# An attention block with a SwiGLU network behind it: matmuls that read their moving operand as two halves in turn

## The chip, the cores and the metric

The kernel runs on one core of a Trainium2 chip. A core has TensorE (matmuls, which read SBUF and write PSUM), VectorE, ScalarE and GpSimd, which work on their own and wait for each other through semaphores, and queues that issue DMAs. The metric is the time of one execution on the device, in microseconds. Times given are medians of several runs; the profile is of one execution.

## The reference

Two blocks follow each other. The first lets 32 inducing points attend to a sequence, and then the sequence to the result; the second is an RMS norm with a gated network.

```python
# x: (4, 12416, 128), inducing: (32, 128)
def mab(q, kv):
    s = (q @ kv.transpose(0, 2, 1)) / sqrt(128)
    a = exp(s - s.max(-1, keepdims=True))
    a /= a.sum(-1, keepdims=True) + 1e-09
    return a @ kv
h = mab(inducing, x)           # (4, 32, 128)
y = mab(x, h)                  # (4, 12416, 128), then (49664, 128)

# w_gate, w_val: (128, 1536), w_out: (1536, 128)
xn = y / sqrt(mean(y * y, -1) + 1e-06) * rms_g
g, val = xn @ w_gate, xn @ w_val
out = (g * (1 / (1 + exp(-g))) * val) @ w_out
```

All is float32.

## The kernel before

The output of the attention is never formed. Since y = a @ h, the product xn @ w_gate is a @ (h * rms_g @ w_gate), with the norm's factor put into the weights a. For each of the 4 batches the kernel makes the two small products of h with w_gate and w_val, 32 rows each. It stacks them four times (two upper and two lower parts of the numbers) into the tiles `sg` and `sv`, 128 x 1536, of type float32r. The attention weights, turned so that tokens lie along the columns, are likewise split into an upper and a lower part, and `gather` copies these into the tile `a` of a unit: 128 partitions by T tokens.

A **unit** is T tokens: 512 in 80 of the 100 units, 480 in 16, 256 in 4. There are 25 units in a batch. `ffn(b, u)` makes the steps of one unit, and each unit has 12 **slots**, one for each 128 of the 1536 hidden columns. A slot `j` (function `slot`) does:

- the gate product (L732), `sg` stationary and `a` moving, into one of five PSUM banks `gv`; ScalarE takes SiLU of it into `silu` (L740);
- the value product (L743) into another of these banks; VectorE multiplies both (L749) into the factor, either in place in PSUM or into a tile `u` in SBUF.

The factor then goes to the output product with `w_out`, which adds up over the 12 slots in the PSUM tile `acc`. It goes one of two ways, chosen in advance for each slot by a table of letters (619 `s`, 200 `d`, 381 dots):

- **plain** (a dot): one float32 matmul `acc += wo[j] x u` (`project`, L669). The trace has two records for each such product.
- **split** (`s` or `d`): the factor is split by ScalarE, VectorE and GpSimd (L714, L715, L718, L719, L723, L724 in `three`) into float32r parts `hi`, `lo` and `d`, and `project3` makes three float32r matmuls: two into the PSUM tile `u3` (L690 and L692), one into `acc` (L669). When the last split product of a unit is done, ScalarE evicts `u3` (L695) into `o`.

At the end of a unit `finish` adds `acc` and `o` (L677, on VectorE), then VectorE turns the sum in blocks of 32 x 32 (L680), and `store` sends the four groups of 32 partitions to the output by DMA. In the two units without a split product there is no L695 and no L677, and L680 reads `acc` itself.

The kernel keeps eight PSUM banks: five `gv`, two `acc`, one `u3`. All loops are unrolled. The order of instructions on each engine is written out by hand: tables say at which slot a step of the next batch's attention is placed, which of the plain (`p`) and split (`t`) output products are issued within which slot, which of the five banks a product takes, and which buffer a factor takes. A scheduler does not reorder anything.

Of the kernel before, what the change touches and what calls it, by code (L numbers as in the profile page):

```python
# [13 lines left out]
AF = mybir.ActivationFunctionType  # L14
ALU = mybir.AluOpType
# [3 lines left out]
P = 128  # L19
R = 4  # L20
# [3 lines left out]
def kernel(  # L24
# [45 lines left out]
    nc = tc.nc  # L70
# [3 lines left out]
    NJ = F // P  # L74
# [421 lines left out]

    split_of, moving = {}, {}

    def seam(b, s):

        st = {}
        n, rows = per2[s], rows2[s]
        w = n * m
        engine = nc.gpsimd if b or s else nc.vector

        def numbers(name):
            return small.tile([P, 16], F32, name=name)[rows, 0:n]

        def turn_a():
            eT = st["eT"] = worker([P, 512], F32, "eT")  # L510
            nc.vector.transpose(out=eT[rows, 0:w], in_=sc[b][rows, cols2[s]])

        def square():
            ps = st["ps"] = bank()
            nc.tensor.matmul(ps[rows, 0:w], gram[b][rows, rows], st["eT"][rows, 0:w], start=True, stop=True)  # L515

        def turn_z():
            ps = st["ps"]
            z = st["z"] = worker([P, 512], F32, "z")[:, 0:n * m].rearrange("p (t m) -> p t m", m=m)
            flat = z[rows, :, :].rearrange("p t m -> p (t m)")  # L520
            nc.vector.tensor_tensor(out=flat, in0=ps[rows, 0:w], in1=st["eT"][rows, 0:w], op=ALU.mult)
            nc.vector.transpose(out=flat, in_=flat)

        def scale():
            ms = numbers("ms")
            nc.vector.reduce_sum(out=least[rows, 0:n, 0], in_=st["z"][rows, :, :], axis=AX.X)
            nc.vector.reduce_max(out=ms, in_=least[rows, 0:n, :], axis=AX.X)
            st["ms"] = ms

        def root():  # L530
            rs = st["rs"] = numbers("rs")
            nc.gpsimd.tensor_tensor(out=rs, in0=st["ms"], in1=mhalf[rows, 0:n], op=ALU.pow)

        def apply():
            rs, a = st["rs"], weights(b, s)
            engine.tensor_tensor(out=a, in0=a, in1=rs.unsqueeze(2).to_broadcast((rs.shape[0], n, m)), op=ALU.mult)

        def turn_b():
            aT = st["aT"] = worker([P, 512], F32, "aT")
            nc.vector.transpose(out=aT[rows, 0:w], in_=sc[b][rows, cols2[s]])  # L540

        def split():
            aT = st["aT"]
            hi, lo = split_of[b, s] = [halves.tile([P, 512], F32R, name=k) for k in ("hi", "lo")]
            if b or s:
                nc.scalar.copy(out=hi[rows, 0:w], in_=aT[rows, 0:w])
            else:
                nc.vector.tensor_copy(out=hi[rows, 0:w], in_=aT[rows, 0:w])
            engine.tensor_tensor(out=lo[rows, 0:w], in0=aT[rows, 0:w], in1=hi[rows, 0:w].bitcast(F32), op=ALU.subtract)

        return [turn_a, square, turn_z, scale, root, apply, turn_b, split]
# [98 lines left out]
    def weight_of(kind, j):  # L650
        if j >= NK:
            return kws["last"][:, kind * (NJ - NK) + j - NK, :]
        n = kind * NK + j
        return kws["first"][:, n, :] if n < half + NK else kws["more"][:, n - half - NK, :]

    def ffn(b, u):

        s, q = units[u]
        T = per2[s] * m
        a = moving.pop((b, u))  # L660
        sg, sv = stacks[b]
        acc = ps_acc.tile([P, 512], F32, name="acc")
        nk = sum((b, u, j) in kinds for j in range(NJ))
        st = {"left": NJ, "k": nk}
        if nk:
            st["o"] = None

        def project(lhsT, rhs):
            nc.tensor.matmul(acc[:, 0:T], lhsT, rhs, start=st["left"] == NJ, stop=st["left"] == 1)  # L669
            st["left"] -= 1  # L670
            if not st["left"]:
                soon(1, finish)

        def finish():
            o = st["o"] if nk else outp.tile([P, 512], F32, name="o")
            if nk:
                nc.vector.tensor_tensor(out=o[:, 0:T], in0=acc[:, 0:T], in1=o[:, 0:T], op=ALU.add)  # L677

            def turn():
                nc.vector.transpose(out=o[:, 0:T], in_=(o if nk else acc)[:, 0:T])  # L680
                soon(2, lambda: store(o))

            soon(1, turn)

        def project3(j, where):
            if st["k"] == nk:
                st["u"] = ps_u.tile([P, 512], F32, name="u3")
            ups = st["u"]
            hi, lo, d = (one[:, 0:T] for one in kws["sets"][where])
            nc.tensor.matmul(ups[:, 0:T], weight_of(0, j), hi, start=st["k"] == nk, stop=False)  # L690
            st["k"] -= 1
            nc.tensor.matmul(ups[:, 0:T], weight_of(1, j), lo, start=False, stop=not st["k"])  # L692
            if not st["k"]:
                o = st["o"] = outp.tile([P, 512], F32, name="o")
                nc.scalar.activation(o[:, 0:T], ups[:, 0:T], AF.Copy, scale=1.0 + 2.0 ** -12)  # L695
            project(weight_of(2, j), d)
            give_back(where, idle, leaving)

        def store(o):
            if s == full:  # L700
                d = out[ds(b * N + start[s], P * per[s]), :].rearrange("(i w) c -> i w c", i=m)
            else:
                d = of(out, b, s)[q]
            for k in range(R):
                queue = nc.scalar if (b, u) == flat[-1] and k % 2 else nc.sync
                queue.dma_start(out=d[:, :, ts(k, m)], in_=o[ts(k, m), 0:T].rearrange("p (t c) -> p t c", c=m))

        def three(j, t):

            where = idle.pop(0)  # L710
            hi, lo, d = (one[:, 0:T] for one in kws["sets"][where])
            v, kind = t[:, 0:T], kinds[b, u, j]
            if kind == "sums":
                nc.scalar.activation(hi, v, AF.Copy, scale=(1.0 - 2.0 ** -13) * 2.0 ** -12)  # L714
                nc.vector.scalar_tensor_tensor(out=lo, in0=hi.bitcast(F32), scalar=-4096.0, in1=v,  # L715
                                               op0=ALU.mult, op1=ALU.add)
            else:
                nc.scalar.activation(d, v, AF.Copy, scale=1.0 - 2.0 ** -13)  # L718
                nc.gpsimd.tensor_tensor(out=lo, in0=v, in1=d.bitcast(F32), op=ALU.subtract)  # L719

            def rest():
                if kind != "sums":
                    nc.scalar.activation(hi, d.bitcast(F32), AF.Copy, scale=2.0 ** -12)  # L723
                nc.gpsimd.tensor_tensor(out=d, in0=hi.bitcast(F32), in1=lo.bitcast(F32), op=ALU.subtract)  # L724
                kara.append(lambda: project3(j, where))

            soon(1, rest)

        def slot(j, products, steps, tanh):
            products(0)  # L730
            g = bank()
            nc.tensor.matmul(g[:, 0:T], sg[:, ts(j, P)], a[:, 0:T], start=True, stop=True)  # L732
            sl = silp.tile([P, 512], F32, name="silu")
            if tanh:

                nc.scalar.activation(sl[:, 0:T], g[:, 0:T], AF.Tanh, scale=0.5)
                nc.vector.scalar_tensor_tensor(out=sl[:, 0:T], in0=sl[:, 0:T], scalar=1.0, in1=g[:, 0:T],
                                               op0=ALU.add, op1=ALU.mult)
            else:
                nc.scalar.activation(sl[:, 0:T], g[:, 0:T], AF.Silu)  # L740
            products(1)
            v = bank()
            nc.tensor.matmul(v[:, 0:T], sv[:, ts(j, P)], a[:, 0:T], start=True, stop=True)  # L743
            t = v if kinds.get((b, u, j)) == "sums" else up.tile([P, 512], F32, name="u", tag=f"u{factors.pop(0)}")
            if tanh:
                nc.vector.scalar_tensor_tensor(out=t[:, 0:T], in0=sl[:, 0:T], scalar=0.5, in1=v[:, 0:T],
                                               op0=ALU.mult, op1=ALU.mult)
            else:
                nc.vector.tensor_tensor(out=t[:, 0:T], in0=sl[:, 0:T], in1=v[:, 0:T], op=ALU.mult)  # L749
            steps()  # L750
            if (b, u, j) in kinds:
                soon(1, lambda: three(j, t))
            else:
                plain.append(lambda: project(wo[:, j, :], t[:, 0:T]))

        return slot
# [550 lines left out]
```

## Time and profile before

| what | value |
|---|---|
| median of 3 runs | 1573.27 us (1573.14 to 1574.48) |
| the profiled execution, its span from the first to the last instruction | 1571.7 us |
| TensorE busy | 1559.7 us, 99% of the span |
| VectorE busy | 1461.7 us, 93% |
| GpSimd busy | 1432.5 us, 91% |
| ScalarE busy | 1302.4 us, 83% |
| granted TensorE clock | 1.000 |
| DMA engines, mean over the span | 72 GB/s |

The profiled execution is known by its span alone; the runs, timed from outside, stand 1.6 us above it at the median. Matmuls are pipelined: the duration of a matmul's record overlaps the next one, so that the pace is read from the distance between the ends of consecutive records, or from the pieces of the chain of waits, which follow one another without overlap. "PEld" is the load of a stationary operand, which lies beside the matmuls. A name such as `xn` can stand for another tile that uses the same buffer: the rings of `hi`, `lo` and `d` lie in buffers that the input used at first, and later in those of `sg` and `sv`.

### The profile page before, as it was taken

The page shows a single profiled execution, that of the slowest core. Times are in us where ns is not written, and L with a number is a line of the kernel's source. Part 1 is how long each engine was busy: PE and PEld are TensorE (multiplying, and loading weights), DVE is VectorE, ACT ScalarE, POOL GpSimd, SP SyncE. Part 2 cuts the span into 40 slices and gives each one's busy share as a digit, 9 for nine tenths or more (in the row PEclk, how much of TensorE's full clock was granted, in tenths as well). Part 3 has the DMA queues.
Part 4 walks back from the last instruction along what each step waited for, and adds up shares of the span by engine and source line. Part 5 has one row for each costly group of instructions (what it writes and reads, how often), then busy time and mean ns, then how long its engine had stood idle before and what let it go on. Part 6 is the DMA issues. An engine that isn't in the chain of part 4 may idle for free.

```text
span 1571.7 us, 26132 instructions
## 1 busy us (share of the span) xinstructions
PE 1559.7 (99%) x7141; PEld 1108.5 (71%) x7141; DVE 1461.7 (93%) x2546; ACT 1302.4 (83%) x2501; POOL 1432.5 (91%) x1158
## 2 busy tenths in 40 slices
PE   9999999999999999999999999999999999999998
PEld 6566667767776667776677667776777777777777
DVE  6999999899999998999999999899999999999997
ACT  5687888788888889887988888978798888888886
POOL 1379999999999999999999999899989999999997
PEclk9999999999999999999999999999999999999999
DMA  7355526334453242634444323353212122121221
GB/s 283 86 87 92 102 40 132 84 65 87 66 93 61 37 91 39 132 81 85 71 77 81 55 60 71 81 109 73 51 36 39 35 36 36 33 37 37 40 39 27
DMA packets 389331, 112.58 MB, mean 72 GB/s; under 512 B 365088, under 2 KB 369728, under 8 KB 386624
## 3 DMA queue, kind: packets, MB, share of 16 engines
q1 hardware_dynamic: 388592, 110.83, 35.4%
q8 instruction: 57, 0.93, 0.3%
q14 instruction: 90, 0.74, 0.2%
q10 hardware_dynamic: 592, 0.08, 0.0%
HBM read 53.95 MB, written 27.00 MB: 52 GB/s over the span
## 4 chain that ended last, share of the span: by engine, by line
PE 97%; DVE 1%; ACT 1%; POOL 0%; issue 0%; DMA 0%; SPq 0%; ACTq 0%; POOLq 0%; DVEq 0%
PE acc L669 31%; PE gv L732 18%; PE gv L743 17%; PE u L690 12%; PE u L692 12%; PE gv L341 3%; PE gv L515 1%; PE gv L390 1%; PE gv L808 1%; PE acc L191 0%; PE gv L469 0%; ACT silu L740 0%; PE gv L483 0%; DVE u L749 0%; DMA out_dram<-o 0%
## 5 line engine op out<-in xcount | busy, mean ns | idle before, releaser
L724 POOL TENSOR_TENSOR xn<-xn,xn 128x512 fp32r<-128x512 f32 (+2 forms) x626 | 776.2, 1259 | 47.2 <-DVE xn L715 13.7
L740 ACT ACTIVATE silu<-gv 128x512 f32<-128x512 f32 (+2 forms) x1186 | 683.7, 587 | 135.3 <-PE gv L732 123.6
L743 PE MATMUL gv<-a,sv 128*128 128x512 f32 (+2 forms) x1188 | 566.3, 477 | 0.0
L732 PE MATMUL gv<-a,sg 128*128 128x512 f32 (+2 forms) x1188 | 481.8, 406 | 0.6 <-ACT silu L740 0.3
L749 DVE TENSOR_TENSOR gv<-silu,gv 128x512 f32<-128x512 f32 (+2 forms) x616 | 412.4, 674 | 35.1 <-PE gv L743 14.1
L749 DVE TENSOR_TENSOR u<-silu,gv 128x512 f32<-128x512 f32 (+2 forms) x570 | 370.5, 656 | 32.4 <-PE gv L743 15.2
L669 PE MATMUL acc<-u,wo 128*128 128x512 f32 (+2 forms) x762 | 370.3, 576 | 0.0
L714 ACT ACTIVATE xn<-gv 128x512 fp32r<-128x512 f32 (+2 forms) x472 | 278.3, 590 | 56.3 <-DVE gv L749 39.4
L715 DVE SCALAR_TENSOR_TENSOR xn<-xn,gv 128x512 fp32r<-128x512 f32 (+2 forms) x472 | 312.9, 663 | 9.4 <-ACT xn L714 4.5
L732 PEld LDWEIGHTS gv<-a,sg 128*128 128x128 f32 x1188 | 223.6, 188 | 132.7 <-issue 32.6
L743 PEld LDWEIGHTS gv<-a,sv 128*128 128x128 f32 x1188 | 223.8, 188 | 106.7 <-issue 26.6
L690 PE MATMUL u<-xn,xn 128*128 128x512 f32 (+2 forms) x599 | 242.3, 405 | 0.0
L669 PE MATMUL acc<-xn,more 128*128 128x512 f32 (+2 forms) x599 | 232.0, 387 | 0.0
L719 POOL TENSOR_TENSOR xn<-u,xn 128x512 fp32r<-128x512 f32 (+2 forms) x154 | 192.4, 1249 | 5.4 <-ACT xn L718 5.3
L669 PEld LDWEIGHTS acc<-u,wo 128*128 128x128 f32 x762 | 142.5, 188 | 43.4 <-issue 16.9
L690 PEld LDWEIGHTS u<-xn,xn 128*128 128x128 f32 x599 | 112.7, 188 | 32.9 <-issue 7.2
L724 POOL TENSOR_TENSOR sg<-sg 128x512 fp32r<-128x512 f32 (+2 forms) x97 | 124.8, 1286 | 5.0 <-DVE sg L715 1.4
L669 PEld LDWEIGHTS acc<-xn,more 128*128 128x128 f32 x599 | 112.5, 188 | 23.5
L724 POOL TENSOR_TENSOR sv<-sv 128x512 fp32r<-128x512 f32 (+1 forms) x96 | 123.5, 1286 | 5.9 <-DVE sv L715 3.2
L692 PE MATMUL u<-xn,more 128*128 128x512 f32 (+2 forms) x304 | 117.3, 386 | 0.0
L692 PE MATMUL u<-xn,xn 128*128 128x512 f32 (+2 forms) x295 | 114.0, 386 | 0.0
L718 ACT ACTIVATE xn<-u 128x512 fp32r<-128x512 f32 (+2 forms) x154 | 95.3, 619 | 12.6 <-DVE u L749 5.2
(231 smaller groups left out, 1921.2 us busy)
## 6 DMA issues: line engine op xcount, KB each, us to landing
out_dram<-o SPq DMA_DIRECT2D x320, 64.0 KB, 2.0
xT<-in_x_dram SPq DMA_DIRECT2D x60, 256.0 KB, 3.8
xn<-in_x_dram SPq DMA_DIRECT2D x60, 256.0 KB, 5.1
a<-hi SPq DMA_DIRECT2D x156, 64.0 KB, 2.0
a<-lo SPq DMA_DIRECT2D x156, 64.0 KB, 2.0
xn<-in_x_dram SPq DMA_DIRECT2D x5, 1024.0 KB, 9.0
xn<-w SPq DMA_DIRECT2D x18, 256.0 KB, 3.0
out_dram<-o SPq DMA_DIRECT2D x64, 60.0 KB, 2.0
```

What stands on the lines that cost most here:

```text
L669: nc.tensor.matmul(acc[:, 0:T], lhsT, rhs, start=st["left"] == NJ, stop=st["left"] == 1)
L690: nc.tensor.matmul(ups[:, 0:T], weight_of(0, j), hi, start=st["k"] == nk, stop=False)
L692: nc.tensor.matmul(ups[:, 0:T], weight_of(1, j), lo, start=False, stop=not st["k"])
L714: nc.scalar.activation(hi, v, AF.Copy, scale=(1.0 - 2.0 ** -13) * 2.0 ** -12)
L715: nc.vector.scalar_tensor_tensor(out=lo, in0=hi.bitcast(F32), scalar=-4096.0, in1=v, op0=ALU.mult, op1=ALU.add)
L718: nc.scalar.activation(d, v, AF.Copy, scale=1.0 - 2.0 ** -13)
L719: nc.gpsimd.tensor_tensor(out=lo, in0=v, in1=d.bitcast(F32), op=ALU.subtract)
L724: nc.gpsimd.tensor_tensor(out=d, in0=hi.bitcast(F32), in1=lo.bitcast(F32), op=ALU.subtract)
L732: nc.tensor.matmul(g[:, 0:T], sg[:, ts(j, P)], a[:, 0:T], start=True, stop=True)
L740: nc.scalar.activation(sl[:, 0:T], g[:, 0:T], AF.Silu)
L743: nc.tensor.matmul(v[:, 0:T], sv[:, ts(j, P)], a[:, 0:T], start=True, stop=True)
L749: nc.vector.tensor_tensor(out=t[:, 0:T], in0=sl[:, 0:T], in1=v[:, 0:T], op=ALU.mult)
```

## The change

Two functions are new. `halves_in_turn` reorders the access pattern of a moving operand: instead of columns 0, 1, 2, ... of T it reads 0, T/2, 1, T/2 + 1, ... . All gate, value and output products use it, plain and split. The result of a product therefore lies in that order in PSUM, and SiLU and the split keep it. The output product reads its operand, which is already in that order, as two halves in turn again, so that the columns of `acc` and `u3` stand as four quarters of the tokens in turn. `in_order` reads such a PSUM tile with a step of four columns, so that it comes out in the order of the tokens: in L695 for `u3`, in L677 for `acc`. In the two units without split products a copy from `acc` to `o` is new, and L680 then reads `o`. The tables of the order of work stay as they are.

```diff
--- before.py
+++ after.py
@@ -496,6 +496,14 @@
 
     split_of, moving = {}, {}
 
+    def halves_in_turn(ap):
+
+        return ap.rearrange("p (h n) -> p n h", h=2)
+
+    def in_order(ap):
+
+        return ap.rearrange("p (n q) -> p q n", q=R)
+
     def seam(b, s):
 
         st = {}
@@ -666,18 +674,21 @@
             st["o"] = None
 
         def project(lhsT, rhs):
-            nc.tensor.matmul(acc[:, 0:T], lhsT, rhs, start=st["left"] == NJ, stop=st["left"] == 1)
+            nc.tensor.matmul(acc[:, 0:T], lhsT, halves_in_turn(rhs), start=st["left"] == NJ, stop=st["left"] == 1)
             st["left"] -= 1
             if not st["left"]:
                 soon(1, finish)
 
         def finish():
             o = st["o"] if nk else outp.tile([P, 512], F32, name="o")
+            whole = o[:, 0:T].rearrange("p (q n) -> p q n", q=R)
             if nk:
-                nc.vector.tensor_tensor(out=o[:, 0:T], in0=acc[:, 0:T], in1=o[:, 0:T], op=ALU.add)
+                nc.vector.tensor_tensor(out=whole, in0=in_order(acc[:, 0:T]), in1=whole, op=ALU.add)
+            else:
+                nc.vector.tensor_copy(out=whole, in_=in_order(acc[:, 0:T]))
 
             def turn():
-                nc.vector.transpose(out=o[:, 0:T], in_=(o if nk else acc)[:, 0:T])
+                nc.vector.transpose(out=o[:, 0:T], in_=o[:, 0:T])
                 soon(2, lambda: store(o))
 
             soon(1, turn)
@@ -687,12 +698,13 @@
                 st["u"] = ps_u.tile([P, 512], F32, name="u3")
             ups = st["u"]
             hi, lo, d = (one[:, 0:T] for one in kws["sets"][where])
-            nc.tensor.matmul(ups[:, 0:T], weight_of(0, j), hi, start=st["k"] == nk, stop=False)
+            nc.tensor.matmul(ups[:, 0:T], weight_of(0, j), halves_in_turn(hi), start=st["k"] == nk, stop=False)
             st["k"] -= 1
-            nc.tensor.matmul(ups[:, 0:T], weight_of(1, j), lo, start=False, stop=not st["k"])
+            nc.tensor.matmul(ups[:, 0:T], weight_of(1, j), halves_in_turn(lo), start=False, stop=not st["k"])
             if not st["k"]:
                 o = st["o"] = outp.tile([P, 512], F32, name="o")
-                nc.scalar.activation(o[:, 0:T], ups[:, 0:T], AF.Copy, scale=1.0 + 2.0 ** -12)
+                nc.scalar.activation(o[:, 0:T].rearrange("p (q n) -> p q n", q=R), in_order(ups[:, 0:T]), AF.Copy,
+                                     scale=1.0 + 2.0 ** -12)
             project(weight_of(2, j), d)
             give_back(where, idle, leaving)
 
@@ -729,7 +741,7 @@
         def slot(j, products, steps, tanh):
             products(0)
             g = bank()
-            nc.tensor.matmul(g[:, 0:T], sg[:, ts(j, P)], a[:, 0:T], start=True, stop=True)
+            nc.tensor.matmul(g[:, 0:T], sg[:, ts(j, P)], halves_in_turn(a[:, 0:T]), start=True, stop=True)
             sl = silp.tile([P, 512], F32, name="silu")
             if tanh:
 
@@ -740,7 +752,7 @@
                 nc.scalar.activation(sl[:, 0:T], g[:, 0:T], AF.Silu)
             products(1)
             v = bank()
-            nc.tensor.matmul(v[:, 0:T], sv[:, ts(j, P)], a[:, 0:T], start=True, stop=True)
+            nc.tensor.matmul(v[:, 0:T], sv[:, ts(j, P)], halves_in_turn(a[:, 0:T]), start=True, stop=True)
             t = v if kinds.get((b, u, j)) == "sums" else up.tile([P, 512], F32, name="u", tag=f"u{factors.pop(0)}")
             if tanh:
                 nc.vector.scalar_tensor_tensor(out=t[:, 0:T], in0=sl[:, 0:T], scalar=0.5, in1=v[:, 0:T],
```

## The prediction

> **What bounds the kernel now.** I read the shares of the chain of waits first, then a table of windows, the chain piece by piece, and the groups by form.
>
> ```profile
> span 1571.7 us, 26132 instructions
> ...
> PE 97%; DVE 1%; ACT 1%; POOL 0%; issue 0%; DMA 0%; SPq 0%; ACTq 0%; POOLq 0%; DVEq 0%
> PE acc L669 31%; PE gv L732 18%; PE gv L743 17%; PE u L690 12%; PE u L692 12%; PE gv L341 3%; PE gv L515 1%; PE gv L390 1%; PE gv L808 1%; PE acc L191 0%; PE gv L469 0%; ACT silu L740 0%; PE gv L483 0%; DVE u L749 0%; DMA out_dram<-o 0%
> ```
>
> The chain is TensorE nearly everywhere, and 90% of it is the five lines that the change edits. Who comes next is read from one window, from the first full units to the tail:
>
> ```profile
> core 0: us, PE busy (x) PEld busy (x) DVE busy (x) ACT busy (x) POOL busy (x), PEclk, DMA share, GB/s
> 100.00:1540.00 1440.00, 1439.26 (x6368) 1026.81 (x6367) 1355.12 (x2318) 1216.65 (x2331) 1374.83 (x1097) 1.00 0.35 66
> ```
>
> In these 1440 us GpSimd is idle for 65 us, VectorE for 85, ScalarE for 223. The clock is full, so no gain can come from there. How fast the products go is seen in the chain, where each piece lasts until the next one takes over:
>
> ```profile
> 56.30 1.72 PE acc L669 x4
> ...
> 602.33 0.23 PE gv L743
> 602.56 0.23 PE gv L732
> 602.79 0.23 PE u L690
> 603.03 0.23 PE u L692
> 603.26 0.23 PE acc L669
> ...
> 605.12 0.86 PE acc L669 x2
> ```
>
> Two speeds. A plain fp32 product (L669 on wo) is two records of 0.43 us. A record streams its operand twice (a product is four passes), so a pass of 512 columns takes 0.215. An fp32r product streams it once and takes 0.23. From the ends of consecutive records in the trace (medians): fp32 records 429 ns at 512 columns, 402.5 at 480 and 215.5 at 256, hardly varying (428 to 430 at 512). The fp32r ones take 232.5, 217 and 118, and vary (225 to 240 at 512). So the array shows 214.5, 201 and 108 ns a pass, and fp32r falls 18, 16 and 10 ns short: 8%, in proportion to the columns. It is the same on all five lines (231.5 to 232.9) and whether VectorE, ScalarE, GpSimd or DMAs are busy beside it or not (232.0 to 233.1). So the loss lies in the fp32r pass itself. An fp32r pass takes a new word at every step of the array, a plain record one at every second step. I read the loss as the moving operand arriving too slowly: a reading, not shown.
>
> **The change, part by part.**
>
> *The reads.* The marks in the kernel give 819 split products of 1200, 381 plain. fp32r passes: 2 x 1200 gate and value, 3 x 819 split, 4857 in all. No instruction is added; only the order in which the moving operand is read changes. 80 of 100 units have 512 columns, 16 have 480, 4 have 256, so the shortfall is 0.80 x 18 + 0.16 x 16 + 0.04 x 10 = 17.4 ns a pass, and 4857 x 17.4 ns = 84 us of TensorE time. That is the gain's end. The other end: if the words came at one per two steps, as a plain record takes them, a pass would cost what a plain record does, 429: (196.5 x 0.80 + 185.5 x 0.16 + 97.5 x 0.04) = 191 ns more a pass, 927 us in all. No matmul of the trace reads its operand with a hop, so these rows are bounds. The row of another engine nearest to it is on VectorE:
>
> ```profile
> L715 DVE SCALAR_TENSOR_TENSOR xn<-xn,gv 128x512 fp32r<-128x512 f32 x370 | 251.0, 678 | 6.2 <-ACT xn L714 2.3
> ...
> L677 DVE TENSOR_TENSOR o<-acc,o 128x512 f32<-128x512 f32 x78 | 53.2, 683 | 0.0
> ...
> L279 DVE SCALAR_TENSOR_TENSOR we<-sc,we 128x512 int32<-128x512 int32 x6 | 4.1, 684 | 0.0
> ```
>
> L279 reads every second word of its source and takes 684 ns; L715, the same operation on adjacent words, takes 678. A hop alone costs VectorE nothing there, at half the array's pace or less. Two facts make me take the gain's end: a pass that falls short in proportion to its length with neighbours idle or busy is held up by its own run of addresses, and the change alters just that run; and the one hop on view is free. It is the weakest step here.
>
> Plain records: 762 x 0.43 us already run at the array's pace with a word per two steps, so I cost their new order at nothing; if a hop takes more than two steps, that cover is gone and every nanosecond per pass costs 1.5 us over their 1524 passes.
>
> *A rule against, and one for.* The row: an fp32r pass of adjacent words is 8% slow. The Trainium skill, "SBUF — State Buffer", section "Door 1: The DMA port swizzle", says that a read wants at least two hits on a 16-byte line and pays each time that it moves to another line. In the new order every word lies in another line than the one before, so by the rule alone passes get slower and the sum goes to the rivals below; no run here shows it for TensorE. "Vector Engine (DVE) Microarchitecture Reference", section "5.2 Measured stream behaviour on trn2", speaks for both: 1.73 ns a column where a source of VectorE hops at every word, but the full rate where one stream alternates between two regions, which is this pattern. By its first figure, my estimate is 886 ns a pass and a kernel near 4,700 us; by its second, the forecast.
>
> *What of the 84 us is kept.* A faster TensorE asks the others for more in the same time. In the window it would need 1440 - 83 = 1357 us, VectorE 1355, GpSimd 1375: three engines level, in an order written by hand, with five PSUM banks for gate and value. GpSimd's 1375 caps the gain at 65. What is late next is a split operand from L724 (1297 ns on GpSimd) or a factor from L749. No row gives the share kept; I take half of 65, 33 us, since all three would then still stand at 96 to 98% of 1407 us.
>
> *The evictions.* 98 of 100 units leave `acc` through L677 (683 ns) and `u` through L695 on ScalarE (608 ns); both now read every fourth word of PSUM. By L279 that costs nothing, which I take as the nearest row; the upper end is a doubling: 98 x 0.68 = 67 us on VectorE against its 85 idle, 98 x 0.6 = 59 on ScalarE against 223. Behind L695 waits the next unit's first L690, since `u` has one PSUM bank: now 6.2 us, 19 times, in the table of waits; a doubling could make it 98 x 0.6 = 59 more, of which I allow 27 in the range. The two units without split products (all plain, at the start) get a VectorE copy before their transpose, 2 x 0.69 = 1.4 us, hidden by `acc`'s second bank. Their transpose read from PSUM took 710 ns against 703 from SBUF: nothing.
>
> **Sum.** 1571.7 - 33 = 1538.7 us of span. The runs' median, 1573.27, stands 1.6 above the profiled span, and I carry that: 1540.3. With 65 kept it is 1508; with 33 kept and the evictions' 27 lost, 1567.
>
> **Rivals.**
>
> *The order of reading makes no difference.* Then fp32r stays at 232.5 and only the evictions are left: 1573, to 1600 with their 27 us. For it: a loss that is the same whatever runs beside it could as well be a clock ratio of the port, which no address order cures. Against: such a loss should not vary by 15 ns between passes. 14 in 100, half of it within 0.2% (3.2 us, about what a measurement of this kernel can tell from no change).
>
> *Each change of place costs (slower).* If the 18 ns are the price of moving on in memory, the new order moves more often. Its place is the moving read of the 4857 passes, and no slack hides it, since TensorE is the bound: each further 17.4 ns costs 84 us, and it decides from 0.7 ns a pass (3.2 us). With the loss at two to four times I get 1658 to 1826; the factors are my estimate, without a row. For it: proportion to length and the scatter. Against: L279's free hop. 18 in 100.
>
> *One word per two steps (slower).* The port delivers pairs of adjacent words, and half of each is now thrown away: 191 ns x 4857 = 927 us, 2500 us. For it: 2048 bytes a partition in 230 ns, 8.9 GB/s, is already close to a limit, since the pass falls short of the array. Against: nothing but the forecast's two facts. 18 in 100.
>
> That the change doesn't do what it says is small: the two reorderings make four columns in turn, which the evictions put back.
>
> **How the numbers follow.** Forecast 50 in 100, with 1508 to 1567 its own range. Faster 0.50, the same 0.07; slower 0.07 + 0.18 + 0.18 = 0.43. The range runs from 1505 (the cap of 65 us, and a little from before 100 us) to 1826, the top of the second rival; it leaves out the third, 18 in 100. Cases of both signs hold most of the chance, hence its width.
>
> **What would show it.** Right: ends of consecutive fp32r records 215 to 220 ns apart at 512 columns, fp32 ones still 429; pieces of L732 and L743 at 0.22; VectorE or GpSimd taking a visible share of the chain, and TensorE with idle time before its weight loads; L677 and L695 near 683 and 608. Wrong: fp32r records 250 to 430 apart, with the chain still at 97% TensorE and the other engines idle in proportion; or at 232 with the span unmoved; or L677 over 900 ns and L690 waiting for L695 at most of the 98 unit ends.

## The result, and the profile after

The changed kernel takes **1589.57 us** (median of 4 runs, 1589.52 to 1589.68) against 1573.26 before (1573.14 to 1574.48): a ratio of 1.0102, with a 95% interval of 1.0088 to 1.0117. It is 16 us slower, where 33 us less were forecast. In both profiles a few line numbers differ for the same step: L732 is now L744 (gate), L743 is L755 (value), L690 and L692 are L701 and L703, L669 is L677, L677 is L686, L695 is L706, L680 is L691, L715 is L727, L724 is L736.

The page of the changed kernel: its span, and the chain of waits by engine and by line.

```profile
span 1587.9 us, 26134 instructions
...
PE 96%; DVE 2%; issue 1%; ACT 0%; DMA 0%; POOL 0%; DVEq 0%; ACTq 0%
PE acc L677 35%; PE gv L744 17%; PE gv L755 16%; PE u L701 11%; PE u L703 11%; PE gv L341 3%; PE gv L523 1%; PE gv L390 1%; PE gv L820 1%; PE gv L469 0%; DMA xn<-in_x_dram 0%; DVE gv L761 0%; PE gv L483 0%; DVE xn L727 0%; ACT silu L752 0%
```

TensorE is still the chain. Within it the four lines that hold fp32r products alone have each lost a point of the span, and the line that also holds the plain products has gone from 31 to 35%. The chain piece by piece says why (start, length, engine and line):

```profile
57.12 2.16 PE acc L677 x4
...
607.35 0.22 PE acc L677
607.57 0.22 PE u L701
607.78 0.22 PE u L703
608.00 0.21 PE acc L677
608.21 0.22 PE gv L755
608.43 0.22 PE gv L744
608.64 1.08 PE acc L677 x2
```

The fp32r products have come down from 0.23 to 0.22 or 0.21, and a plain record has gone up from 0.43 to 0.54. The ends of consecutive records give it exactly (medians, 512 columns): fp32r 232.5 to 216 ns, with no scatter left (215 to 216 in the middle nine tenths of the split products, where it was 227 to 237); plain records 429 to 539 (402.5 to 506 at 480 columns, 216 to 270.5 at 256).

Since each record's end follows the one before, the distances between ends add up to the span, but for 6.7 us at its two ends. Sums by kind, in us:

| kind | records | before | after | difference |
|---|---|---|---|---|
| gate | 1200 | 284.1 | 271.1 | -13.0 |
| value | 1200 | 272.4 | 258.0 | -14.4 |
| split output | 2457 | 555.7 | 517.0 | -38.7 |
| plain output | 762 | 315.3 | 396.3 | +81.0 |
| all other matmuls | 1521 | 137.5 | 138.8 | +1.3 |
| sum | | 1565.0 | 1581.2 | +16.2 |

The spans differ by 16.2 as well, 1587.9 less 1571.7. The fp32r passes at their median distances come to 1096.5 before and 1020.0 after, so the faster reading is worth 76.5; 10.4 of it went into TensorE's new waits. The plain records' 81.0 took the rest and more.

The window from the first full units to the tail, and the two evictions, in the groups by form:

```profile
core 0: us, PE busy (x) PEld busy (x) DVE busy (x) ACT busy (x) POOL busy (x), PEclk, DMA share, GB/s
100.00:1556.00 1456.00, 1454.83 (x6385) 1027.45 (x6384) 1360.68 (x2326) 1219.23 (x2338) 1367.89 (x1099) 1.00 0.35 66
```

```profile
L686 DVE TENSOR_TENSOR o<-acc,o 128x512 f32<-128x512 f32 x78 | 53.2, 683 | 0.0
...
L688 DVE COPY o<-acc 128x512 f32<-128x512 f32 x2 | 1.4, 684 | 0.0
```

```profile
L706 ACT ACTIVATE o<-u 128x512 f32<-128x512 f32 x78 | 47.2, 606 | 1.3 <-PE u L703 1.3
```

GpSimd and VectorE do nearly the work of before in a window 16 us longer, so they have become idler, not busier. Reading every fourth column of PSUM costs nothing: 683 ns as before on VectorE, 606 against 608 on ScalarE. The two new copies take 1.4 us in all, as worked out.

### The profile page after: what moved, and what is told of

It is laid out like the page before. It is cut to its first block, busy times and chain, and to the rows that moved or that the text cites. A ratio compares the mean times of both kernels' runs of the same rounds, so it can differ in the third digit from the quotient of the medians.

```text
span 1587.9 us, 26134 instructions
## 1 busy us (share of the span) xinstructions
PE 1574.8 (99%) x7141; PEld 1105.1 (70%) x7141; DVE 1463.7 (92%) x2548; ACT 1301.3 (82%) x2501; POOL 1421.5 (90%) x1158
## 4 chain that ended last, share of the span: by engine, by line
PE 96%; DVE 2%; issue 1%; ACT 0%; DMA 0%; POOL 0%; DVEq 0%; ACTq 0%
PE acc L677 35%; PE gv L744 17%; PE gv L755 16%; PE u L701 11%; PE u L703 11%; PE gv L341 3%; PE gv L523 1%; PE gv L390 1%; PE gv L820 1%; PE gv L469 0%; DMA xn<-in_x_dram 0%; DVE gv L761 0%; PE gv L483 0%; DVE xn L727 0%; ACT silu L752 0%
## 5 line engine op out<-in xcount | busy, mean ns | idle before, releaser
L736 POOL TENSOR_TENSOR xn<-xn,xn 128x512 fp32r<-128x512 f32 (+2 forms) x626 | 769.2, 1248 | 62.1 <-DVE xn L727 25.5
L755 PE MATMUL gv<-a,sv 128*128 128x512 f32 (+2 forms) x1188 | 580.6, 489 | 0.1
L744 PE MATMUL gv<-a,sg 128*128 128x512 f32 (+2 forms) x1188 | 469.3, 395 | 0.9 <-ACT silu L752 0.4
L677 PE MATMUL acc<-u,wo 128*128 128x512 f32 (+2 forms) x762 | 451.8, 684 | 0.0
L761 DVE TENSOR_TENSOR gv<-silu,gv 128x512 f32<-128x512 f32 (+2 forms) x616 | 412.1, 674 | 38.7 <-PE gv L755 18.0
L761 DVE TENSOR_TENSOR u<-silu,gv 128x512 f32<-128x512 f32 (+2 forms) x570 | 370.7, 656 | 42.4 <-PE gv L755 23.6
L744 PEld LDWEIGHTS gv<-a,sg 128*128 128x128 f32 x1188 | 224.4, 189 | 153.3 <-issue 28.3
L727 DVE SCALAR_TENSOR_TENSOR xn<-xn,gv 128x512 fp32r<-128x512 f32 (+2 forms) x472 | 312.9, 663 | 10.1 <-ACT xn L726 5.1
L755 PEld LDWEIGHTS gv<-a,sv 128*128 128x128 f32 x1188 | 224.6, 189 | 133.9 <-ACT silu L752 35.2
L701 PE MATMUL u<-xn,xn 128*128 128x512 f32 (+2 forms) x599 | 236.9, 395 | 0.0
L677 PE MATMUL acc<-xn,more 128*128 128x512 f32 (+2 forms) x599 | 223.0, 372 | 0.0
L677 PEld LDWEIGHTS acc<-u,wo 128*128 128x128 f32 x762 | 143.3, 190 | 41.1 <-issue 23.7
L701 PEld LDWEIGHTS u<-xn,xn 128*128 128x128 f32 x599 | 113.3, 189 | 27.2 <-issue 9.1
L736 POOL TENSOR_TENSOR sg<-sg 128x512 fp32r<-128x512 f32 (+2 forms) x97 | 123.5, 1273 | 6.8 <-DVE sg L727 2.1
L736 POOL TENSOR_TENSOR sv<-sv 128x512 fp32r<-128x512 f32 (+1 forms) x96 | 122.3, 1273 | 6.7 <-DVE sv L727 2.2
L677 PEld LDWEIGHTS acc<-xn,more 128*128 128x128 f32 x599 | 113.3, 189 | 14.6 <-POOL xn L736 0.7
L703 PE MATMUL u<-xn,more 128*128 128x512 f32 (+2 forms) x304 | 113.0, 372 | 0.0
L703 PE MATMUL u<-xn,xn 128*128 128x512 f32 (+2 forms) x295 | 109.8, 372 | 0.0
```

The costliest lines, as they stand in the source:

```text
L677: nc.tensor.matmul(acc[:, 0:T], lhsT, halves_in_turn(rhs), start=st["left"] == NJ, stop=st["left"] == 1)
L701: nc.tensor.matmul(ups[:, 0:T], weight_of(0, j), halves_in_turn(hi), start=st["k"] == nk, stop=False)
L703: nc.tensor.matmul(ups[:, 0:T], weight_of(1, j), halves_in_turn(lo), start=False, stop=not st["k"])
L744: nc.tensor.matmul(g[:, 0:T], sg[:, ts(j, P)], halves_in_turn(a[:, 0:T]), start=True, stop=True)
L755: nc.tensor.matmul(v[:, 0:T], sv[:, ts(j, P)], halves_in_turn(a[:, 0:T]), start=True, stop=True)
```

## The experiments

Theory A: the change did two things that nearly cancel, a gain on fp32r passes and a loss on plain fp32 records, each where the moving operand is read. Its rival, theory B: the gain was there to be had, but the order written by hand no longer fits a faster TensorE. The first three runs are to part the two.

**1. Only gate and value read halves in turn.**

```diff
-nc.tensor.matmul(acc[:, 0:T], lhsT, halves_in_turn(rhs), ...)
+nc.tensor.matmul(acc[:, 0:T], lhsT, rhs, ...)
 ... (hi and lo likewise; in_order and its results with q=2)
```

> Only the gate and value products read halves in turn; all output products read adjacent words, and the evictions take every second column. Theory A (the new order brings every fp32r pass to the array's pace, about 16 ns less at 512 columns, and slows only plain fp32 records, by 110 ns each): 2400 fp32r passes save about 39 us, plain records stay at 429 ns, a little is lost to waits: 1535 to 1545 us. Theory B (the gain is used up because the order written by hand no longer fits a faster TensorE, whatever the plain records do): 1565 to 1580 us, with the weight loads waiting for ScalarE and VectorE much longer than before.

Measured: 1551.04 us against 1573.22, a ratio of 0.9859 (0.9844 to 0.9874). Plain records stand at 429 ns and gate and value at 216, as theory A has it. The range of A was missed by 6 us: gate and value save 28 us of the 39, since their own waits grew, the split products give back 4, and the other matmuls 2. Theory B's time is excluded, but it is right in that more is lost to waits than I allowed. In its chain, a plain record and a split pass as before, and between them the shorter gate and value:

```profile
605.67 0.43 PE acc L677
606.10 0.22 PE gv L755
606.31 0.22 PE gv L744
606.53 0.23 PE u L701
```

**2. Only the output products read halves in turn.**

```diff
-nc.tensor.matmul(g[:, 0:T], sg[:, ts(j, P)], halves_in_turn(a[:, 0:T]), start=True, stop=True)
+nc.tensor.matmul(g[:, 0:T], sg[:, ts(j, P)], a[:, 0:T], start=True, stop=True)
 ... (v likewise; in_order and its results with q=2)
```

> Only the output products, plain and split, read halves in turn; gate and value read adjacent words, and the evictions take every second column. Theory A: 2457 split passes save about 38 us, 762 plain records at 539 instead of 429 ns cost 81: 1610 to 1622 us. Theory B: plain records cost little of the end, the time stays within 1565 to 1590.

Measured: 1615.97 us, a ratio of 1.0271 (1.0256 to 1.0286), within A's range. The plain records cost 81.2 us more than before and the split products 39.2 less; the span is 42.8 longer. So the loss stands on its own, without any change to gate and value. The two parts' spans, 21.6 shorter and 42.8 longer, add up to 21 us, near the 16 of the whole change. In its chain, a gate product and a plain one:

```profile
607.10 0.23 PE gv L744
607.33 1.08 PE acc L677 x2
```

**3. The change, with plain products read in a row.** They read adjacent words and write every second column of `acc`, which puts the columns where the change had them; `straight` is set for the plain products alone.

```diff
+to, rhs = ((acc[:, 0:T].rearrange("p (n h) -> p h n", h=2), rhs.rearrange("p (h n) -> p h n", h=2))
+           if straight else (acc[:, 0:T], halves_in_turn(rhs)))
-nc.tensor.matmul(acc[:, 0:T], lhsT, halves_in_turn(rhs), ...)
+nc.tensor.matmul(to, lhsT, rhs, ...)
```

> As the change, but a plain fp32 product reads its operand as adjacent words and writes every second column of acc, so that the columns of acc stand in the same order as in the change. Theory A: plain records back at 429 ns, fp32r passes at 216; the change's loss of 81 us goes away and 10 to 25 us of the gain are lost to waits: 1508 to 1525 us, with GpSimd nearly always busy. Theory A': the hop costs a plain record the same on the side where it writes PSUM: records at about 539 ns, about 1590 us. Theory B: records at 429 ns and yet 1550 us or more, since the others can't follow.

Measured: **1539.90 us** (1539.79 to 1540.28), a ratio of 0.9788 (0.9773 to 0.9802): faster than both kernels. Here are its span and its window, and a plain product in its chain:

```profile
span 1538.5 us, 26134 instructions
```

```profile
100.00:1507.00 1407.00, 1402.69 (x6373) 1012.22 (x6372) 1349.13 (x2320) 1207.28 (x2332) 1361.18 (x1096) 1.00 0.36 68
```

```profile
593.13 0.21 PE gv L757
593.34 0.22 PE gv L746
593.56 0.87 PE acc L679 x2
594.43 0.04 issue
594.47 1.27 POOL xn L738
```

Plain records are back at 429 ns with their results written to every second column, so their loss in the change is wholly on the side of the reading, and A' falls. fp32r stays at 216. Of theory A the time was missed: 33 us of the 77 reach the end, not 48 to 65. The time lies between A's range and B's: A has the two kinds of record right, but more than half of the gain is lost to waits, which is what B was about. The chain now leaves TensorE for GpSimd in places, as in the last two lines. By kind, gate saves 3 us, value 5 and the split products 27: gate and value run 45 us over their medians for waits, against 15 before, the split products 12 against 1.

**4 to 8. Other orders of reading**, all of them on all products. They ask what it is about the order that helps one kind and hurts the other.

```diff
-return ap.rearrange("p (h n) -> p n h", h=2)
+return ap.rearrange("p (h n k) -> p n h k", h=2, k=2)      # pairs; fours: k=4
+return ap.rearrange("p (n h k) -> p n k h", h=2, k=4)      # near
+return ap.rearrange("p (h n) -> p n h", h=4)               # quarters
+return ap.rearrange("p (n h k) -> p n k h", h=4, k=4)      # near quarters
 ... (the evictions undo each)
```

Pairs:

> As the change, but two adjacent words of each half in turn in place of one (0, 1, T/2, T/2+1, 2, 3, ...). If plain records lose because a lone word of each place is read, they are back at 429 ns and, if it is the change of place that helps fp32r, those stay near 216: 1508 to 1525 us. If what costs plain records is any change of place, they lie between 429 and 539 (about 480, 1545 us). If fp32r needs single words in turn, its passes are at 225 to 232 with plain at 429: about 1573 us.

Two neighbouring runs of four:

> As the change, but the two runs read in turn are neighbours of four words (0, 4, 1, 5, 2, 6, 3, 7, 8, 12, ...). Theory C (even and odd places of the moving stream of an fp32r pass are fetched along two lines of their own, which get in each other's way only when both are in the same small run of memory, and are slow when one line jumps): fp32r at 216 ns or a little above, since each line reads four words in a row; plain records, which fetch one word at a time, jump at every word: about 540 or more. Theory D (what helps is distance, half a tile): fp32r at 230 or more.

Fours:

> As the change, but four adjacent words of each half in turn. Theory C: each of the two lines of an fp32r pass moves to another place after every second word, as it does with adjacent words, only farther: 232 ns, if a far move costs what a near one does, and up to 330 (the pairs) if it costs more; plain records move after four words, 429 to 440. Theory E (any change of place costs, at so many ns each): between 328 at two words and 232, near 280, plain near 440.

Quarters:

> As the change, but with four quarters in turn (0, T/4, T/2, 3T/4, 1, ...), one word of each; the evictions take every sixteenth column. Theory C: even places now jump between the first and third quarter, odd ones between the second and fourth, at every fetch, as with the pairs: fp32r near 328 ns, plain records, one word per place as in the change, near 540. Theory F (single words in turn are good for fp32r, however many places): 216.

Four neighbouring runs of four:

> As the change, but four neighbouring runs of four words in turn, one word of each (0, 4, 8, 12, 1, 5, ...); twice this order is the order of the columns again, so the evictions read adjacent columns. If the number of places in turn counts and not their distance, as with the halves (216 and 542 near, 216 and 539 far): about 278 ns for fp32r and 870 for plain records, 2105 us. If the distance of a quarter of the tile made the quarters slow: nearer 216 and 540.

Measured (the fp32r pass and the plain record at 512 columns, medians, and a range where the five lines differ; for the three kernels of the first experiments see there):

| order of the moving operand | fp32r, ns | plain, ns | time, us | ratio to before, interval |
|---|---|---|---|---|
| adjacent (before) | 232.5 | 429 | 1573.3 | 1 |
| one word of two halves (the change) | 216 | 539 | 1589.57 | 1.0102 (1.0088 to 1.0117) |
| one word of two neighbouring runs of 4 | 216 | 542 | 1590.65 | 1.011 (1.009 to 1.013) |
| four words of two halves | 246 to 254 | 429 | 1651.33 | 1.0496 (1.0475 to 1.0517) |
| two words of two halves | 328 | 453 | 2038.49 | 1.2956 (1.2934 to 1.2978) |
| one word of four quarters | 275 to 283 | 871 | 2105.48 | 1.3382 (1.3355 to 1.3409) |
| one word of four neighbouring runs of 4 | 269 | 907 | 2089.89 | 1.328 (1.3254 to 1.3307) |

In the chain, the two neighbouring runs of four, then the pairs and the quarters:

```profile
608.74 0.22 PE gv L744
608.96 1.08 PE acc L677 x2
```

```profile
621.14 0.33 PE gv L744
621.47 1.81 PE acc L677 x4
```

```profile
621.28 0.27 PE gv L744
...
622.12 2.01 PE acc L677 x3
```

What follows: the distance between the places matters little (216 and 542 with places 4 words apart, 216 and 539 with 256; 269 and 907 against 280 and 871 for four places). For plain records, it is how many places take turns and how many words are read at each: two places one word each 539, four places 871, two words 453, four words 429 as with adjacent ones. For fp32r it is not that: one word of two places is its best, two words of two places its worst. So the pairs, from which I hoped for both, came out slowest but two. Theory D (distance) and theory F (single words are good, however many places) are refuted. Theory C, that even and odd places of an fp32r stream are fetched along two lines, holds for the two neighbouring runs and for the fours, but not for the quarters: it said 328 and 540 and got 280 and 871, and had given the plain records no reason to get slower than with two places. What the fetch really does stays open. Theory E's 280 for four words was too high.

**9 to 11. Who holds back the rest of the shorter passes.** All on the version of experiment 3; some work that the result needs is left out of GpSimd, of VectorE, and of both, so that the times show what holds the kernel back and are no faster kernel. The buffers left half unwritten are filled with zeros first, 6 to 11 us of GpSimd's time.

```diff
-nc.gpsimd.tensor_tensor(out=d, in0=hi..., in1=lo..., op=ALU.subtract)
+nc.gpsimd.tensor_tensor(out=d[:, 0:T // 2], in0=hi...[:, 0:T // 2], in1=lo...[:, 0:T // 2], op=ALU.subtract)
...
-nc.vector.scalar_tensor_tensor(out=lo, in0=hi..., scalar=-4096.0, in1=v, ...)
+nc.vector.scalar_tensor_tensor(out=lo[:, 0:T // 2], in0=hi...[:, 0:T // 2], scalar=-4096.0, in1=v[:, 0:T // 2], ...)
```

> The version with plain products read in a row, and GpSimd subtracts only the first half of the columns of each factor's third part (L736 of the change, 819 times); the other half holds old numbers and the output is not the reference's. If GpSimd's cap is what holds back the 43 us of the 77 us of shorter passes that didn't reach the end (1540 now), the time falls to 1500 to 1515 us. If the order written by hand, ScalarE or VectorE hold them back, it stays at 1530 to 1540.

> The version with plain products read in a row, and VectorE makes only the first half of the columns of the lower part (L727 of the change, 619 times, some 0.26 us less each); the other half holds old numbers and the output is not the reference's. If VectorE's load (96% of the window in the version without this edit) holds back the rest of the shorter passes, the time falls from 1540 to 1500 to 1515 us. If each factor's own chain through ScalarE and VectorE back to a PSUM bank, or the order written by hand, holds it back, it falls by 15 us at most.

> Both reliefs at once: GpSimd's third part and VectorE's lower part only for the first half of the columns (the output is not the reference's). GpSimd's alone gave 4 us. If the two engines stand in for each other as the bound, both together give much more than the sum of the two alone: below 1505 us. If not, about the sum.

Measured: GpSimd relieved 1536.01 us (ratio to before 0.9765, 0.9749 to 0.9781), VectorE relieved 1528.85 (0.9716, 0.9700 to 0.9733), both 1513.90 (0.9622, 0.9608 to 0.9636). Against 1539.90 that is 4, 11 and 26 us. The windows, in that order, with the columns as above:

```profile
100.00:1500.00 1400.00, 1396.50 (x6363) 1013.81 (x6363) 1345.17 (x2316) 1204.36 (x2328) 957.16 (x1103) 1.00 0.36 68
```

```profile
100.00:1495.00 1395.00, 1388.72 (x6372) 1020.37 (x6371) 1227.76 (x2321) 1204.60 (x2333) 1362.88 (x1101) 1.00 0.36 68
```

```profile
100.00:1480.00 1380.00, 1378.82 (x6381) 1027.70 (x6382) 1229.14 (x2325) 1203.80 (x2337) 962.80 (x1105) 1.00 0.36 69
```

Neither engine alone is the bound, and both times fell in the second of their two expected cases. With GpSimd at 957 of 1400 us nearly nothing is won; with VectorE at 1228 of 1395 the split products wait for GpSimd instead (their waits grow from 12 to 22 us). Both together give more than the sum, 26 against 15, though not the "below 1505" of the expectation. So the two stand in for each other in part. Even so, 17 us are missing from the span that 77 us less would give (1512.0 against 1495). In that run gate and value products run 26 us over their medians, 11 more than before the change, and all other matmuls take 4 us more. The weight loads' waits name these, and then the same two waits for SiLU in the kernel before:

```profile
PEld gv L750 <- issue: 32.3, 132, 0.8
PEld gv L761 <- ACT silu L758: 28.4, 98, 1.6
...
PEld gv L750 <- ACT silu L758: 24.4, 85, 0.9
...
PEld gv L750 <- DVE u L767: 14.3, 44, 0.8
```

```profile
PEld gv L743 <- ACT silu L740: 17.6, 66, 0.8
PEld gv L732 <- ACT silu L740: 17.4, 60, 0.8
```

A line gives the total, the times and the longest; L750 and L761 are the gate and the value product, L758 is SiLU, L767 VectorE's multiply. The waits for SiLU have grown from 35 to 53 us, so what is left may mostly be the way of a factor through ScalarE back to its PSUM bank. That is a reading of the waits: no run relieves ScalarE, and a new order of work was not tried.

## Why the prediction was wrong

**The step that failed is the cost of the plain records.** The prediction put it: "Plain records: 762 x 0.43 us already run at the array's pace with a word per two steps, so I cost their new order at nothing; if a hop takes more than two steps, that cover is gone and every nanosecond per pass costs 1.5 us over their 1524 passes." The condition came true. A pass went from 214.5 to 269.5 ns, 55 ns more at 512 columns, and over all forms the records cost 81.0 us (the rule of 1.5 us a nanosecond gives 84). The price stood in the text, but the sum had nothing for it, no rival was made of it, and the forecast's own range, 1508 to 1567, had no room for it. That 1589.6 lies in the wide range up to 1826 is luck: the part above 1567 was there for costly evictions and slower fp32r passes. Experiments 2 and 3 show the loss by itself: it comes without any change to gate and value, and goes when plain products alone read adjacent words.

The argument was a false one. A word per two steps looked like slack, so that the kind that asks for words at half the pace seemed safe. No row showed that slack: the same text has a record stream its operand twice, and two readings of 512 words in 429 ns are a word at every step. The runs show the opposite of what was argued: in the same order fp32r takes a new word every 0.42 ns (216 / 512). A plain record takes one every 1.05 ns (539 / 512), or every 0.53 if it reads its operand twice; no run settles which. Why words of two places in turn slow a plain record stays open.

**The reads.** The mechanism was right: the loss of 8% lies in the fp32r pass itself, comes from the order of its addresses, and goes away with halves in turn. The size: 76.5 us against 84 worked out, 216 ns a pass against 214.5. But that another order would be a better one did not follow from this, and there luck helped: of the six orders tried four are slower for fp32r than adjacent words (246 to 328 ns against 232.5), and the free hop on VectorE foretold none of these losses.

**What is kept.** In the version of experiment 3, where the plain records pay nothing, 33.2 us of the span reach the end, which is what the prediction took (half of GpSimd's 65). The time forecast, 1540.3, is that version's 1539.9 and not the change's. The share of a half had no row behind it, so that it fits so well is luck. Its reason was only half right: relieving GpSimd alone gives 4 us, relieving VectorE with it 26, and 17 us more are lost elsewhere, most of them at gate and value. In the change itself more was kept, 66 of the 76.5 us by the table of sums against 36 in experiment 3: there the fp32r products run 26 us over their medians, in experiment 3 56 us. I read it as the slow plain records giving the other engines time to follow. So gain and loss do not simply add up, and undoing a loss of 81 us brought 50 (1589.57 to 1539.90).

**The evictions.** Right: free, by the row of VectorE's hop, and so is reading every sixteenth column (684 ns on VectorE with the quarters).

**The rivals.** None of the three is what happened. "Order makes no difference" has the measured time in its range (1573 to 1600) for a wrong reason; fp32r did change. "Each change of place costs" is false in this order for the fp32r passes, where I had put it. Plain records do get slower, where I hadn't, but not by a price for each change: two places and four both change at every word, for 539 and 871 ns. "One word per two steps" is refuted (216 ns, not 429).

**The rules.** With halves in turn, fp32r reads each word from another place than the last and is faster for it (216 against 232.5), and with two adjacent words at a time it is slowest (328). So the rule of "SBUF — State Buffer", section "Door 1: The DMA port swizzle", that a read wants at least two hits on a line, does not describe an fp32r pass; it does give the direction for plain records (539, 453 and 429 ns for one, two and four words at a place). The other page, "Vector Engine (DVE) Microarchitecture Reference", section "5.2 Measured stream behaviour on trn2", has the full rate for one stream of VectorE that alternates between two regions. On TensorE fp32r agrees (216 ns against 214.5 for the array's pace), plain records don't (539 against 429).

## What to carry to other kernels

An edit that is applied to all of one line may reach two kinds of instruction: cost each kind by itself, and put an unknown cost of the second kind into the sum with both ends, even where its pace seems to leave room. When a large change moves the time little, add up the distances between the ends of the bound engine's records by kind, before and after; here one table showed that -66 and +81 had met. Then undo the loss where it arises: plain products read in a row and write with a step, and the change becomes worth 2.1%.

## What the runs showed of the hardware that was not expected

- A plain fp32 matmul slows down when words of two places take turns (429 to 539 ns at 512 columns) and more with four (871 to 907), while an fp32r one speeds up with two (232.5 to 216) and slows with four (268 to 283). The distance between the places changes this by about 4% at most.
- Two adjacent words of each place in turn are the worst order tried for fp32r, 328 ns.
- A plain fp32 matmul that writes every second column of a PSUM bank takes what one that writes adjacent columns takes, 429 ns. For fp32r products this was not tried.
- VectorE and ScalarE read every fourth or sixteenth column of PSUM at the pace of adjacent ones (683 and 684 ns; 606 and 601).
